# Weight fetches per attention step, route operations behind x, two low halves on GpSimd: one change to a fused attention and mixture-of-experts kernel

## The chip, the cores and the metric

The kernel runs on one core of a Trainium2 chip. The metric is the device time of one execution in microseconds (us). Engines are named as in the profile: PE is TensorE (PEld its weight loads), DVE VectorE, ACT ScalarE, POOL GpSimd, SP SyncE, which issues most of the DMAs.

## The reference

Eight heads of windowed attention (four plain, four dilated by 4, 32 keys for each query) give x, 4608 tokens of 512. Each token then goes to one of 4 groups and one of 4 experts of its group, and its output row is the expert's two-layer FFN times the two gate weights. Cut to what matters:

```python
scores = np.where(masks, q @ k.T / 8, -1e9)             # 8 batches, 8 heads, 576 positions, 64 wide
x = (softmax(scores) @ v)                               # -> (4608, 512)
g_idx = argmax(x @ w_group); g_w = softmax(x @ w_group)[g_idx]
e_idx = argmax(x @ w_expert[g]); e_w = softmax(...)[e_idx]
out[token] = g_w * e_w * (relu(x @ w1[g, e]) @ w2[g, e])   # w1: 512x1024, w2: 1024x512, 16 experts
```

## The kernel before, in words

**Attention** runs in 36 steps (s = 0 to 35, three lagging ones behind), each 64 queries of two batches with all heads; three steps make a group g, nine a pair of batches bp. A step is a pipeline over engines: scores s on PE (mask matmul L253, then 32 small ones L272), maximum mx and difference d on DVE (L282, L284), exp on ACT, transposition t on PE with its copy pt on ACT, the product with the values o on PE (`av`, two steps later, L314), then den, its reciprocal and x = o / den on DVE (`normalise`, L363 to L370), transposition tx and copies xT on ACT. The accumulator of o has one buffer (pool psA), so the next o waits until x has read it. x goes to a table xd in memory (`store_x`); q, k and v of the coming groups are loaded by SP (`load_q`, `load_k` in two halves, `load_v`).

**Routing.** When a pair of batches is through, `turned_logits` forms its logits on PE and `route(bp)`, a generator, picks group and expert of each token, ranks the tokens, and writes slots, tables and gates. Its some 40 DVE operations are small, most 0.2 to 0.35 us. `slot()` is called after each large DVE operation of a step and lets route run on as far as a credit allows. The last things of a route are the gate weights gt (`L554` on ACT, stored by SP at L556), the table of tokens and, for two of the routes, `find`, whose entry list lets GpSimd gather rows of an early expert (`fetch_rows`, tiles xe, L687). Route 2 also picks the second early expert (`pick`).

**Early experts.** The two fullest experts so far are picked after routes 1 and 2, and some of their tokens (128 and 256) are computed while attention and the last route end. `prefetch` drives `load_weights`: the expert's w1 and w2 are 8 chunks of 512 KB. A chunk is fetched by SP into one of four stage buffers w (L641), multiplied by 64 into fp16 by ACT (the high half, L662), and the rest, the low half, is formed either on DVE in one operation (L659) or on GpSimd in two (multiply L656, subtract L657). A chunk's stage buffer is free for the fetch four chunks later when its low half is done; expert 1's chunks 0 to 3 thus take the buffers of expert 0's chunks 4 to 7. `WSTEPS` says how many such pieces run in a step (1 unless named), `EARLY_STEPS` the same for the first expert's FFN, `TAIL` the order of the pieces after the attention loop: r is a piece of the last route, a of expert 0's FFN, b of expert 1's, w of the weights. After that come 16 pieces of experts, whose order is fixed too.

**Order.** PE, DVE, ACT and SP execute what stands here in the order of the code; GpSimd's order is the scheduler's. Each queue is served in order, so an instruction that waits holds all behind it. In the built program SP's transfers use eight semaphores in turn, and each transfer waits until the one eight places ahead of it has landed.

Of the kernel before, what the change touches and what calls it, by code (L numbers as in the profile page):

```python
# [26 lines left out]
NT = NBP * NJ  # L27
# [13 lines left out]
NEARLY = 2  # L41
NWST = 4
RATE = (0.25, 0.3, 0.4)
WSTEPS = {NT - 9: 1, NT - 8: 0, NT + 1: 2, NT + 2: 0}
EARLY_STEPS = {NT - 1: 1, NT: 2, NT + 1: 1}
TAIL = "ararrrarrawrrrawrwarrrrrrwbwarbrwbrrwbrrrwbrrrTwbbb"
NR = NE + NEARLY
# [4 lines left out]
NW = 8192 // WCH  # L52
# [3 lines left out]
def moe_attention_kernel(ctx, tc, q, k, k0, v, cmask, wgate, wpack, out):  # L56
# [174 lines left out]
    routes, gate, credit, rate = [], [], [0.0], [0.0]  # L231
# [5 lines left out]
        for i in range(n):  # L237
            nc.tensor.matmul(t[:, i % 2].rearrange("p (u m c) -> p u m c", u=2, m=2), idb, m, start=True, stop=True)

    def slot():  # L240
        credit[0] = min(credit[0] + rate[0], 2 * rate[0])
        while routes and not gate and credit[0] > 0:
            took = run(routes)
            if took in (2, 3):
                gate.append(took)
            elif took not in (None, 1):
                credit[0] -= took

    def scores(n):
        g, jl, J = n // 3, n % 3, n % NJ  # L250
        s = psS.tile([P, 4, 2, 64], F32, name="s", tag="s")
        m = masks[:, MASK_OF.get(J, 1), :]
        nc.tensor.matmul(  # L253
            s.rearrange("p (t u) w k -> p t (u w) k", t=2),
            idb,
            m.rearrange("p (t k) -> p t k", t=2).unsqueeze(2).broadcast_to([P, 2, 4, 64]),
            start=True,
            stop=False,
        )
        if n < 2:  # L260
            keep_busy((3, 10)[n])
        qv = qb[three(g)][:, jl]
        if n == 0:
            kv, ev0 = k0t[:, :, 0 : 8 * 96].rearrange("p w (s b k) -> p w b s k", s=8, k=32), 2
        else:
            kv, ev0 = kb[g % NK].rearrange("p w (b s k) -> p w b s k", s=8, k=32), 4
        for c in range(4):
            for bb in range(2):
                for a in range(2):
                    sl, j = bb * 4 + c, bb * 2 + a  # L270
                    first, step = jl + a, ev0 - a
                    nc.tensor.matmul(  # L272
                        s[32 * j : 32 * j + 32, c].rearrange("p w k -> p (w k)"),
                        qv[:, (sl * 2 + a) * 32 : (sl * 2 + a) * 32 + 32],
                        kv[:, :, first : first + step + 1 : step, sl],
                        start=False,
                        stop=(c == 3),
                    )
        s = s.rearrange("p c w k -> p (c w) k")
        d = ap.tile([P, 4, 64, 2], F32, name="d", bufs=2)  # L280
        mx = ap.tile([P, 8], F32, name="mx")
        nc.vector.tensor_reduce(mx, s, axis=AX.X, op=ALU.max)  # L282
        slot()
        nc.vector.tensor_tensor(  # L284
            d.rearrange("p c k w -> p c w k"),
            s.rearrange("p (c w) k -> p c w k", w=2),
            mx.rearrange("p (c w) -> p c w", w=2).unsqueeze(3).broadcast_to([P, 4, 2, 64]),
            ALU.subtract,
        )
        slot()  # L290
        dd[n] = d

    def softexp(n):
# [65 lines left out]
    def normalise(n):  # L359
        o = oo.pop(n)  # L360
        ov = o[:, :, 0:260].rearrange("p k (s c) -> p k s c", c=65)
        den = ap.tile([P, 2, 4], F32, name="den")
        nc.vector.tensor_scalar_add(den, ov[:, :, :, 64], 1e-9 / SX)  # L363
        slot()
        nc.vector.reciprocal(den, den)
        slot()
        if n % 3 == 0:
            xg[n // 3] = ap.tile([P, 3, 512], F32, name="x", bufs=2)
        x = xg[n // 3][:, n % 3]
        nc.vector.tensor_tensor(  # L370
            x.rearrange("p (k s c) -> p k s c", k=2, s=4),
            ov[:, :, :, 0:64],
            den.unsqueeze(3).broadcast_to([P, 2, 4, 64]),
            ALU.mult,
        )
        if n % 3 == 2:
            if n < NT - 1:
                store_x(n // 3, (0,))
        elif n % 3 == 0 and n:
            store_x(n // 3 - 1, (1,))  # L380
        st[n] = x.rearrange("p (s w c) -> p s w c", s=4, w=2)
# [247 lines left out]
        nc.vector.tensor_copy(ordi[:, NEARLY:NE], ordf[:, NEARLY:NE])  # L629


    def load_weights(ev, w, aside=lambda i: False):
        src = wpack[bass.ds(ev * P, P), :]

        w32s, depth = {}, len(stages)

        def fetch(i):
            if i < NW:
# [8 lines left out]
        def chunk(i):  # L647
# [4 lines left out]
            if i > 0:  # L652
                w32 = w32s.pop(i - 1)
                h, l = parts(i - 1)
                if aside(i - 1):
                    nc.gpsimd.tensor_scalar(w32, w32, SW, 1.0, ALU.mult, ALU.mult)  # L656
                    nc.gpsimd.tensor_tensor(l, w32, h, ALU.subtract)  # L657
                else:
                    nc.vector.scalar_tensor_tensor(l, w32, SW, h, ALU.mult, ALU.subtract)  # L659
                fetch(i + depth - 1)  # L660
            if i < NW:
                nc.scalar.mul(parts(i)[0], w32s[i], SW)  # L662

        return [lambda i=i: chunk(i) for i in range(-1, NW + 1)]

    def select(ent, which, k0, nt, two):
        sq = sm.tile([P, nt, NE], F32, name=f"sel{nt}")
# [229 lines left out]
    ev, found = {}, []  # L897
# [11 lines left out]
    def prefetch():  # L909
        for r in range(NEARLY):  # L910
            while r not in ev:
                yield
            todo.extend(load_weights(ev[r], wsets[r], lambda i: r == 0 and i not in (4, 6)))
            todo.pop(0)()
            yield
            while not wsets[r]:
# [328 lines left out]
```

## Time and profile before

| | |
|---|---|
| median of 3 runs | 568.92 us (567.52 to 569.07) |
| the profiled execution | 562.74 us |
| its span, first to last instruction | 561.0 us |
| granted clock of PE over the span | 0.996 |
| busy, share of the span | PE 535.4 us (95%), PEld 69%, DVE 66%, ACT 57%, POOL 40% |
| moved by DMA | 134.31 MB, mean 239 GB/s |

The busy share is a mean over stages of different kinds: attention to about 147 us, the early experts with the last route to about 187 us, then the 16 pieces. [...] A releaser is inferred: the engine named is the one that came last by the profile.

### The profile page before, as it was taken

The numbers are of one execution on the slowest core, as the hardware profiler recorded it, in microseconds if no ns is written. First come the engines' busy times: TensorE is split into PE (matmuls) and PEld (weight loads), VectorE is DVE, ScalarE is ACT, GpSimd is POOL, SyncE is SP. The second block draws the span as 40 slices with busy tenths as digits, with TensorE's granted clock in tenths as the row PEclk, the third lists the DMA queues.
The fourth block names the chain that finished last, engine by engine and source line by source line (L and its number), as shares of the span: only waits on it lengthen the run. The fifth ranks groups of instructions, "written<-read, shape, count | busy, mean of one in ns | idle before, by whom it ended". The sixth has DMA issues, their size and how long they took to land.

```text
span 561.0 us, 16459 instructions
## 1 busy us (share of the span) xinstructions
PE 535.4 (95%) x6577; PEld 385.9 (69%) x6577; DVE 370.7 (66%) x846; ACT 317.1 (57%) x563; POOL 223.2 (40%) x211
## 2 busy tenths in 40 slices
PE   6899989997798999999999999999999999999995
PEld 3688878776676676556666666675766756787893
DVE  8776876876777336473868596757657667658650
ACT  6565546575555236464646564656656747647741
POOL 6796665758731423302231614133251421221212
PEclk9999999998999999999999999999999999999999
DMA  8988998798393726958697778779798798897731
GB/s 286 395 285 278 331 275 282 231 315 275 103 316 107 252 68 167 295 162 230 193 292 187 261 193 276 181 249 280 233 302 230 251 327 218 287 327 238 264 103 31
DMA packets 79265, 134.31 MB, mean 239 GB/s; under 512 B 42988, under 2 KB 52630, under 8 KB 79186
## 3 DMA queue, kind: packets, MB, share of 16 engines
q1 hardware_dynamic: 72258, 113.65, 65.7%
q0 software_dynamic: 6784, 19.51, 10.6%
q8 instruction: 53, 0.87, 0.6%
q14 instruction: 26, 0.21, 0.1%
q10 hardware_dynamic: 144, 0.07, 0.0%
HBM read 106.16 MB, written 19.29 MB: 224 GB/s over the span
## 4 chain that ended last, share of the span: by engine, by line
PE 82%; DMA 6%; DVE 5%; issue 2%; ACT 2%; SPq 2%; POOLq 0%; ACTq 0%; DVEq 0%
PE a L748 32%; PE y L841 26%; PE o L314 4%; PE y L859 4%; PE s L272 4%; DMA qb<-q 4%; PE yt L876 3%; PE t L302 3%; DMA kb<-k 2%; PE tx L392 2%; SPq L357 1%; PE lt_ps L417 1%; PE s L253 1%; DMA w<-wpack 1%; DVE wb2l L659 1%
## 5 line engine op out<-in xcount | busy, mean ns | idle before, releaser
L812 POOL DMA_INDIRECT out<-yr,sent x31 | 34.4, 1109 | 220.3 <-ACT yr L811 204.0
L756 DVE SCALAR_TENSOR_TENSOR hl<-a,hh 128x256 f16<-128x256 f32 (+13 forms) x144 | 61.1, 425 | 91.5 <-ACT hh L755 91.3
L748 PE MATMUL a<-xs,wb1h 128*128 128x256 f16 (+7 forms) x576 | 97.8, 275 | 2.5 <-DVE hl L756 2.5
L748 PE MATMUL a<-xs,wa 128*128 128x304 f16 (+7 forms) x864 | 96.6, 272 | 0.0
L755 ACT ACTIVATE hh<-a 128x256 f16<-128x256 f32 (+13 forms) x144 | 55.8, 388 | 63.0 <-PE a L748 62.2
L748 PEld LDWEIGHTS <-wa 128*128 128x128 f16 x864 | 79.2, 98 | 16.4 <-issue 0.2
L841 PEld LDWEIGHTS <-hh 128*128 128x128 f16 x480 | 46.9, 98 | 54.8 <-issue 1.2
L659 DVE SCALAR_TENSOR_TENSOR wa<-w,wa 128x1024 f16<-128x1024 f32 x58 | 69.5, 1217 | 19.1 <-ACT wa L662 19.1
L748 PE MATMUL a<-xs,wb1l 128*128 128x256 f16 (+7 forms) x288 | 78.3, 275 | 0.0
L841 PE MATMUL y<-wa,hh 128*128 128x512 f16 x240 | 73.9, 379 | 0.0
L662 ACT ACTIVATE wa<-w 128x1024 f16<-128x1024 f32 x64 | 66.8, 1055 | 1.5 <-DMA w<-wpack 1.3
L748 PEld LDWEIGHTS <-wb1h 128*128 128x128 f16 x576 | 55.1, 98 | 15.2 <-issue 3.0
L811 ACT ACTIVATE yr<-y,cs 128x512 f32<-128x512 f32 (+3 forms) x31 | 21.3, 687 | 64.4 <-issue 32.1
L687 POOL DMA_INDIRECT xr<-xd,sent x41 | 41.9, 1022 | 29.9 <-DVE sent L675 16.7
L659 DVE SCALAR_TENSOR_TENSOR wb2l<-w,wb2h 128x1024 f16<-128x1024 f32 x32 | 38.3, 1219 | 17.1 <-ACT wb2h L662 17.1
L303 ACT COPY pt<-t 128x512 f32<-128x512 f32 x36 | 21.1, 586 | 44.7 <-PE t L302 44.4
L841 PE MATMUL y<-wb2h,hh 128*128 128x512 f16 x120 | 45.6, 380 | 0.0
L841 PE MATMUL y<-wb2h,hl 128*128 128x512 f16 x120 | 45.5, 379 | 0.0
L841 PE MATMUL y<-wb2l,hh 128*128 128x512 f16 x120 | 45.5, 379 | 0.0
L841 PE MATMUL y<-wa,hl 128*128 128x512 f16 x120 | 45.5, 379 | 0.0
L314 PE MATMUL o<-vs,pt 128*32 128x130 f32 x576 | 40.4, 278 | 3.8 <-POOL wa L657 1.4
L282 DVE TENSOR_REDUCE mx<-s 128x8 f32<-128x512 f32 x36 | 24.6, 685 | 25.0 <-PE s L272 24.8
(206 smaller groups left out, 1073.1 us busy)
## 6 DMA issues: line engine op xcount, KB each, us to landing
w<-wpack SPq DMA_DIRECT2D x128, 512.0 KB, 5.1
kb<-k SPq DMA_DIRECT2D x24, 384.0 KB, 4.6
vt<-v SPq DMA_DIRECT2D x14, 390.0 KB, 7.1
qb<-q SPq DMA_DIRECT2D x7, 768.0 KB, 6.2
xd<-x SPq DMA_DIRECT2D x24, 192.0 KB, 5.8
wa<-v SPq DMA_DIRECT2D x6, 390.0 KB, 7.5
wa<-q SPq DMA_DIRECT2D x3, 768.0 KB, 8.6
xd<-x SPq DMA_DIRECT2D x32, 48.0 KB, 4.4
```

The costliest lines, as they stand in the source:

```text
L272: nc.tensor.matmul(s[32 * j : 32 * j + 32, c].rearrange("p w k -> p (w k)"), qv[:, (sl * 2 + a) * 32 : (sl * 2 + a) * 32 + 32], kv[:, :, f ...
L282: nc.vector.tensor_reduce(mx, s, axis=AX.X, op=ALU.max)
L314: nc.tensor.matmul(o[32 * j : 32 * j + 32, c // 2, at : at + 130], pt[n % NPT][:, c, 32 * j : 32 * j + 32], t[:, :, jl, bb * 4 + c, :], st ...
L659: nc.vector.scalar_tensor_tensor(l, w32, SW, h, ALU.mult, ALU.subtract)
L662: nc.scalar.mul(parts(i)[0], w32s[i], SW)
L687: nc.gpsimd.indirect_dma_start(out=xr[0:n], out_offset=None, in_=xd[0:known, :], in_offset=bass.IndirectOffsetOnAxis(ap=ent[0:n, t : t + 1 ...
L748: nc.tensor.matmul(a[:, 0:cap], ww[:, c * FF + f * P : c * FF + f * P + P], xx[:, c, 0:cap], start=(i == 0), stop=(i == len(mm) - 1),)
L755: nc.scalar.activation(hh[:, f, 0:cap], a[:, 0:cap], AF.Relu)
L756: nc.vector.scalar_tensor_tensor(hl[:, f, 0:cap], a[:, 0:cap], 0.0, hh[:, f, 0:cap], ALU.max, ALU.subtract)
L812: ins = nc.gpsimd.indirect_dma_start(out=out, out_offset=bass.IndirectOffsetOnAxis(ap=ent[0:n, t : t + 1], axis=0), in_=yr[0:n, :], in_off ...
L841: nc.tensor.matmul(yp, h[:, f, t * P : t * P + n], ww[:, f * DM : f * DM + DM], start=(i == 0), stop=(i == len(mm) - 1),)
L859: nc.tensor.matmul(yp[q * (P // g) : q * (P // g) + n, 0:wd], h[:, f, t * P : t * P + n], ww[:, f * DM + q * wd : f * DM + q * wd + wd], s ...
```

## The change

Three things change. Expert 0's weights are no longer fetched four at once in step 27 and one per step from step 30 on; `load_weights` with ahead=2 fetches chunk 0 in step 27, chunk 1 in step 28 and from then on the chunk two places ahead of the one that ACT multiplies. The step without a piece is 34 in place of 28, and step 38 now has one, so the first four fetches of expert 1 are written in step 38 in place of 37. `slot(hold)` lets nothing run in scores from step 34 on and in normalise of steps 34 and later (n of 32 and more); what is owed is run at the slot behind normalise. And chunks 4 and 5 of expert 1 form their low halves on GpSimd, where all eight were on VectorE; expert 0's six stay there.

```diff
--- before.py
+++ after.py
@@ -41,7 +41,9 @@
 NEARLY = 2
 NWST = 4
 RATE = (0.25, 0.3, 0.4)
-WSTEPS = {NT - 9: 1, NT - 8: 0, NT + 1: 2, NT + 2: 0}
+HOLD = NT - 2
+ASIDE = ((0, 1, 2, 3, 5, 7), (4, 5))
+WSTEPS = {NT - 9: 1, NT - 2: 0, NT + 1: 2, NT + 2: 1}
 EARLY_STEPS = {NT - 1: 1, NT: 2, NT + 1: 1}
 TAIL = "ararrrarrawrrrawrwarrrrrrwbwarbrwbrrwbrrrwbrrrTwbbb"
 NR = NE + NEARLY
@@ -237,8 +239,15 @@
         for i in range(n):
             nc.tensor.matmul(t[:, i % 2].rearrange("p (u m c) -> p u m c", u=2, m=2), idb, m, start=True, stop=True)
 
-    def slot():
-        credit[0] = min(credit[0] + rate[0], 2 * rate[0])
+    owed = [0]
+
+    def slot(hold=False):
+
+        owed[0] += 1
+        if hold:
+            return
+        n, owed[0] = owed[0], 0
+        credit[0] = min(credit[0] + n * rate[0], (n + 1) * rate[0])
         while routes and not gate and credit[0] > 0:
             took = run(routes)
             if took in (2, 3):
@@ -280,14 +289,14 @@
         d = ap.tile([P, 4, 64, 2], F32, name="d", bufs=2)
         mx = ap.tile([P, 8], F32, name="mx")
         nc.vector.tensor_reduce(mx, s, axis=AX.X, op=ALU.max)
-        slot()
+        slot(n >= HOLD)
         nc.vector.tensor_tensor(
             d.rearrange("p c k w -> p c w k"),
             s.rearrange("p (c w) k -> p c w k", w=2),
             mx.rearrange("p (c w) -> p c w", w=2).unsqueeze(3).broadcast_to([P, 4, 2, 64]),
             ALU.subtract,
         )
-        slot()
+        slot(n >= HOLD)
         dd[n] = d
 
     def softexp(n):
@@ -361,9 +370,9 @@
         ov = o[:, :, 0:260].rearrange("p k (s c) -> p k s c", c=65)
         den = ap.tile([P, 2, 4], F32, name="den")
         nc.vector.tensor_scalar_add(den, ov[:, :, :, 64], 1e-9 / SX)
-        slot()
+        slot(n >= HOLD - 2)
         nc.vector.reciprocal(den, den)
-        slot()
+        slot(n >= HOLD - 2)
         if n % 3 == 0:
             xg[n // 3] = ap.tile([P, 3, 512], F32, name="x", bufs=2)
         x = xg[n // 3][:, n % 3]
@@ -629,10 +638,11 @@
         nc.vector.tensor_copy(ordi[:, NEARLY:NE], ordf[:, NEARLY:NE])
 
 
-    def load_weights(ev, w, aside=lambda i: False):
+    def load_weights(ev, w, aside=lambda i: False, ahead=None):
         src = wpack[bass.ds(ev * P, P), :]
 
         w32s, depth = {}, len(stages)
+        lead = ahead or depth - 1
 
         def fetch(i):
             if i < NW:
@@ -657,11 +667,13 @@
                     nc.gpsimd.tensor_tensor(l, w32, h, ALU.subtract)
                 else:
                     nc.vector.scalar_tensor_tensor(l, w32, SW, h, ALU.mult, ALU.subtract)
-                fetch(i + depth - 1)
+            if i > 0 or ahead:
+                fetch(i + lead)
             if i < NW:
                 nc.scalar.mul(parts(i)[0], w32s[i], SW)
 
-        return [lambda i=i: chunk(i) for i in range(-1, NW + 1)]
+        whole = [lambda i=i: chunk(i) for i in range(-1, NW + 1)]
+        return [lambda i=i: fetch(i) for i in range(ahead)] + whole[1:] if ahead else whole
 
     def select(ent, which, k0, nt, two):
         sq = sm.tile([P, nt, NE], F32, name=f"sel{nt}")
@@ -910,7 +922,7 @@
         for r in range(NEARLY):
             while r not in ev:
                 yield
-            todo.extend(load_weights(ev[r], wsets[r], lambda i: r == 0 and i not in (4, 6)))
+            todo.extend(load_weights(ev[r], wsets[r], lambda i: i in ASIDE[r], 2 - 2 * r))
             todo.pop(0)()
             yield
             while not wsets[r]:
```

SP, from step 27 on: w is a weight chunk, qb, kb queries and keys of the last group, xd the stores of x and of the gates gt (the ISA row ahead of each w is left out). Before:

```order
L110 DMA qb_108<-q 128x512
L641 DMA w_2174<-wpack 128x1024
L641 DMA w_2176<-wpack 128x1024
L641 DMA w_2178<-wpack 128x1024
L641 DMA w_2180<-wpack 128x1024
L110 DMA qb_108<-q 128x512
L345 DMA xd<-x 64x3x256
L350 DMA xd<-x 48x256
L357 DMA xd<-x 48x2x256
L357 DMA xd<-x 16x3x256
L556 DMA xd<-gt 128x9x16
L114 DMA kb_115<-k 64x1536
```

Now:

```order
L112 DMA qb_108<-q 128x512
L651 DMA w_2174<-wpack 128x1024
L112 DMA qb_108<-q 128x512
L354 DMA xd<-x 64x3x256
L359 DMA xd<-x 48x256
L366 DMA xd<-x 48x2x256
L366 DMA xd<-x 16x3x256
L565 DMA xd<-gt 128x9x16
L651 DMA w_2272<-wpack 128x1024
L116 DMA kb_115<-k 64x1536
```

Three fetches have moved: the second stands behind gt, the third ahead of the last half of kb, the fourth behind the values that follow it.

VectorE, step 34, with route 2 picking the second early expert (own, km, top, ordi are its small tiles). Before:

```order
L282 TENSOR_REDUCE mx<-s 128x8
L577 SCALAR_TENSOR_TENSOR own<-own,low 128x16
L580 SCALAR_TENSOR_TENSOR own<-top,own 128x16
L284 TENSOR_TENSOR d<-s,mx 128x4x2x64
L583 TENSOR_REDUCE km<-own 128x1
L585 TENSOR_TENSOR top<-own,km 128x16
L363 TENSOR_SCALAR den<-o 128x8
L587 TENSOR_TENSOR own<-top,own 128x16
L589 TENSOR_REDUCE km<-own 128x1
L591 CAST ordi<-km 128x1
L593 TENSOR_TENSOR own<-top,own 128x16
L365 RECIPROCAL den<-den 128x8
```

Now:

```order
L291 TENSOR_REDUCE mx<-s 128x8
L293 TENSOR_TENSOR d<-s,mx 128x4x2x64
L372 TENSOR_SCALAR den<-o 128x8
L374 RECIPROCAL den<-den 128x8
L379 TENSOR_TENSOR x<-o,den 128x512
L586 SCALAR_TENSOR_TENSOR own<-own,low 128x16
L589 SCALAR_TENSOR_TENSOR own<-top,own 128x16
L592 TENSOR_REDUCE km<-own 128x1
L594 TENSOR_TENSOR top<-own,km 128x16
L596 TENSOR_TENSOR own<-top,own 128x16
```

The five operations of the attention step now stand together, and all of the route's of this step behind x, ahead of the next mx.

GpSimd, at the end of the attention: chunk 7 of expert 0, the two gathers of expert 1's rows (xe, which read xd), the last route's okm and mv, and the first store of finished rows. Before:

```order
L656 TENSOR_SCALAR w_2681<-w_2681 128x1024
L657 TENSOR_TENSOR wa_92<-w_2681,wa_92 128x1024
L687 DMA xe_224<-xd,ente_231 128x528
L687 DMA xe_225<-xd,ente_231 128x528
L509 TENSOR_TENSOR okm<-okm,mine_214 128x72
L512 TENSOR_TENSOR mv<-E_209,okm 128x576 x2
L812 DMA out<-yr,ente_230 4608x512
L687 DMA xr<-xd,sent 128x528
```

Now:

```order
L699 DMA xe_224<-xd,ente_231 128x528
L666 TENSOR_SCALAR w_2850<-w_2850 128x1024
L699 DMA xe_225<-xd,ente_231 128x528
L667 TENSOR_TENSOR wa_92<-w_2850,wa_92 128x1024
L518 TENSOR_TENSOR okm<-okm,mine_214 128x72
L521 TENSOR_TENSOR mv<-E_209,okm 128x576 x2
L666 TENSOR_SCALAR w_3182<-w_3182 128x1024
L824 DMA out<-yr,ente_230 4608x512
L667 TENSOR_TENSOR wb2l<-w_3182,wb2h 128x1024
L666 TENSOR_SCALAR w_3199<-w_3199 128x1024
L667 TENSOR_TENSOR wb2l<-w_3199,wb2h 128x1024
L699 DMA xr<-xd,sent 128x528
```

Chunk 7's two operations have gone behind the first gather and around the second, and four new ones (wb2l, chunks 4 and 5 of expert 1) stand ahead of the gathers xr. The order of TensorE's instructions is the same in both; on ScalarE the multiplications of chunks 5, 6 and 7 each come one step later, that of chunk 7 now behind gt.

## Rows read from the trace of the kernel before

**Rows 1.** Windows: stretch, length, busy us (instructions) by engine, PEclk, DMA share, GB/s

```profile
112.00:187.00 75.00, 64.87 (x998) 50.60 (x990) 54.77 (x162) 41.53 (x84) 40.94 (x31) 0.98 0.67 215
187.00:561.00 374.00, 368.25 (x3355) 253.10 (x3353) 231.44 (x445) 210.39 (x346) 103.04 (x99) 1.00 0.76 227
...
115.00:120.00 5.00, 4.64 (x119) 4.08 (x119) 3.38 (x9) 2.89 (x6) 1.06 (x2) 1.00 0.96 331
...
131.00:132.00 1.00, 1.00 (x25) 1.00 (x21) 0.58 (x1) 0.00 (x0) 0.93 (x1) 0.50 1.03 328
```

**Rows 2.** TensorE's waits, 112 to 187 us: releaser, us in total, times, longest

```profile
PE a L748 <- DVE hl L756: 2.5, 3, 1.2
PE s L272 <- DMA kb<-k: 2.3, 1, 2.3
PE tx L392 <- DVE own L559: 1.5, 1, 1.5
PE o L314 <- POOL wa L657: 1.4, 1, 1.4
PE o L314 <- DVE own L497: 0.9, 1, 0.9
```

**Rows 3.** Timeline of VectorE: start, duration, line, operation, tiles [idle before, releaser]

```profile
136.47 0.69 DVE L282 TENSOR_REDUCE mx<-s 128x8 f32<-128x512 f32 x1 [0.54 <-PE s L272]
...
140.48 1.23 DVE L659 SCALAR_TENSOR_TENSOR wa<-w,wa 128x1024 f16<-128x1024 f32 x1
...
144.18 0.69 DVE L370 TENSOR_TENSOR x<-o,den 128x512 f32<-128x512 f32 x1 [0.17 <-DMA xd<-x]
...
150.99 0.59 DVE L541 TENSOR_SCALAR s<-s 128x45 f32<-128x45 f32 x1
...
172.16 0.19 DVE L541 TENSOR_SCALAR s<-s 128x45 f32<-128x45 f32 x1
```

**Rows 4.** Timeline of SP's DMA issues, 111 to 127 us

```profile
111.69 2.15 SPq L641 DMA_DIRECT2D w<-wpack  x4
...
126.32 0.49 SPq L114 DMA_DIRECT2D kb<-k  x1
```

**Rows 5.** The tile kb, 95 to 150 us, its transfers

```profile
DMA to landing us min/median/max: 3.4/3.6/4.3
```

**Rows 6.** Timeline of TensorE: masks of steps 32, 33, 34; t of step 35

```profile
124.01 0.38 PE L253 MATMUL s<-masks,idb 128*128 128x512 bf16 x1
...
127.15 0.38 PE L253 MATMUL s<-masks,idb 128*128 128x512 bf16 x1
...
135.01 0.38 PE L253 MATMUL s<-masks,idb 128*128 128x512 bf16 x1
...
146.43 0.66 PE L302 MATMUL t<-id,d 128*128 128x128 f32 x4 [0.31 <-DVE xs L725]
```

**Rows 7.** Timeline of SP's DMA issues, 152 to 165 us

```profile
152.87 0.38 SPq L556 DMA_DIRECT2D xd<-gt  x1
...
155.79 0.58 SPq L345 DMA_DIRECT2D xd<-x  x1
...
164.40 0.36 SPq L641 DMA_DIRECT2D w<-wpack  x1
```

**Rows 8.** Timeline of GpSimd, 140 to 157 us

```profile
140.86 1.76 POOL L656 TENSOR_SCALAR w<-w 128x1024 f32<-128x1024 f32 x1 [1.41 <-ACT wa L662]
...
150.21 1.33 POOL L656 TENSOR_SCALAR w<-w 128x1024 f32<-128x1024 f32 x1 [2.94 <-ACT wa L662]
...
155.91 1.09 POOL L687 DMA_INDIRECT xe<-xd,ente  x1 [2.16 <-DVE hl L756]
```

**Rows 9.** Timeline of ScalarE, 168 us: chunk 4 of expert 1

```profile
168.05 1.06 ACT L662 ACTIVATE wb2h<-w 128x1024 f16<-128x1024 f32 x1 [2.54 <-DMA w<-wpack]
```

**Rows 10.** Lines 656 and 657: duration ns min/median/max, first and last start

```profile
L656 POOL TENSOR_SCALAR w<-w x6: 1037/1055/1757, 118.9 to 150.2; 128x1024 f32<-128x1024 f32 x6
...
L657 POOL TENSOR_TENSOR wa<-w,wa x6: 2124/2135/2153, 120.0 to 151.6; 128x1024 f16<-128x1024 f32 x6
```

## The prediction

> **What bounds the kernel now.** I read the stretches first. From 187 us on TensorE is busy 368.25 of 374 us [rows 1]: there it is the bound, and a shift of what stands before 187 us comes out at the end one to one. Between 112 and 187 us it is busy 64.87 of 75 us [rows 1], so 10.1 us at most are to be had, and the change touches this stretch alone. The list of TensorE's waits there [rows 2] has five large entries: 2.5 us for the low halves hl of the early experts' first layer, 2.3 for keys (kb), 1.5, 1.4 and 0.9 around x. The two named "own" and "POOL wa" are, by the program, waits for x: psA has one buffer, so the o of a step can't start before the x of the step before has been read out of it. The x of 144.18 us ends at 144.87 [rows 3], and the o named for 1.4 us starts 0.15 us later.
>
> Two chains cross here. The attention chain ends at the store of the gates of route 2 (gt, L556). Behind that store, in order on SP, stand the first four fetches of early expert 1, and the conversion of its chunks bounds TensorE up to 181 us. So I follow gt, not TensorE, through the change.
>
> **Part 1, one fetch per step.** In before, four fetches go out from 111.69 us on [rows 4]. SP's transfers use eight semaphores in turn, each waiting for the landing of the one eight places earlier; so what follows waits for chunk after chunk, and the second half of the last keys leaves only at 126.32 [rows 4]. It lands some 3.4 us later (3.4 to 4.3 is the spread, [rows 5]) and TensorE waits 2.3 us for it [rows 2]. After that idle time the granted clock is 0.50 at 131 to 132 us [rows 1], the lower of the two levels. Step 33 thus takes 7.86 us from mask to mask, where step 32 took 3.14 [rows 6]: 4.7 more, 2.3 of it the wait, about 1.6 the low clock (some three us at 0.5 to 0.7), the rest the matmuls of the rank, which step 32 doesn't have. In the new order three fetches (1.5 MB) are gone from ahead of the first kb half, one only stands between it and the second, and each of the issues costs SP about 0.55 us as before. I put the second half's issue at 122.5 to 123.5 and its landing at 126 to 128; step 33 wants it at 127.5. The wait is then 0 to 0.8 us. I take 0.4, and the low clock gone: **-3.5 us** at step 34 (bounds -4.0 and, if it lands no earlier, 0). What covers the fetches: each chunk is multiplied by ScalarE two steps after its fetch is written, and SP runs one to two steps behind TensorE, so chunks 2 to 4 may come up to 1.5 us after ScalarE is ready for them; the pt copy queued behind that multiply has 0.8 to 1 us of slack before the o that needs it, since the next scores stand ahead of that o. I cost it at nothing, up to 0.6 us if late. The stage buffers allow it: low 0 is done before chunk 4 is fetched.
>
> **Part 2, route operations behind x.** In step 34 eleven small operations that stood between mx and x now stand behind x, with two that were there already. The o that follows gains the 0.9 us. But the thirteen, 0.2 us each, are all ahead of the next mx: mx of step 35 comes 0.1 + 0.8 + 0.6 + 0.2 + 0.2 + 0.6 + 2.6 = 5.1 us after the scores (the distances of mx, d, den, rec, x and thirteen small ones), no earlier than now, while the 1.23 us low half of 140.48 [rows 3] and two more route operations leave the way of the x behind it. From the mx of step 34 at 136.47 [rows 3] to the t of step 35 at 146.43 [rows 6] it was 9.96 us; in the new order I add up 9.45: **-0.5 us**, not the 2.6 us that the waits sum to, because VectorE's 5.1 us per step are more than TensorE's 3.14. From that t to the gt store at 152.87 it is 6.44 us [rows 6, 7]; x goes first now, but the sums for gt follow it, and the low half that stood ahead of them (1.2) goes behind: no difference. The 1.5 us before tx disappears, yet what it fed (the last logits) is not late next. gt thus leaves at 152.87 - 4.0 = 148.9.
>
> **Part 3, what stands behind gt.** SP: fetches 1 to 3 of expert 1, then fetch 4, whose stage buffer is that of chunk 7 of expert 0. In before that chunk's multiply ran at 150.21 and its subtract right behind it [rows 8], done at 153.7, so all four were out before the store of 155.79 [rows 7]. In the new order chunk 7's two GpSimd operations stand behind the first gather of expert 1's rows and around the second. That gather started 3.04 us after the gt store (152.87 to 155.91, [rows 7, 8]), it has to see the gates landed, and this doesn't change. So: 148.9 + 3.0, gather 1.2, multiply 1.05, 0.3 of issue, second gather 1.0, subtract 2.14 [rows 10], with 0.2 of gaps = 157.8 us for fetch 4, against some 155.3: **2.5 us later although gt is 4 earlier**. Behind it SP has eight stores of x, 0.6 us each [rows 7], then chunk 4 of expert 1: 157.8 + 0.5 + 4.9 + 0.2 = 163.4. In before it left at 164.40, held by the landing of the first store of 155.79, eight places ahead, which lay behind 2 MB of weights. Now only 0.5 MB lies ahead of that store, so the issue time decides: **-1.0 us**. ScalarE waited for this chunk until 168.05 [rows 9], 3.65 us after its fetch, and the first relu of expert 1 stands behind that on ScalarE, ahead of everything that TensorE waits for next; it moves by -0.9. That expert 1's first fetches are now written in step 38 changes nothing: they stand behind gt on SP either way.
>
> **Part 4, two low halves on GpSimd.** VectorE gives up 2 x 1.2 = 2.4 us between 170 and 174 us; GpSimd takes on 2 x (1.055 + 2.135) = 6.4 us [rows 10], from about 168 to 176, where it was idle and before its gathers of the next rows. If the engines didn't touch, TensorE's 2.5 us of waits for hl would shrink only by 0.4: the gt of route 3 and then chunk 7's multiply still stand ahead of the fourth relu on ScalarE. But they do touch. GpSimd's multiply of 140.86 took 1.76 us instead of 1.055 while VectorE's low half of 140.48 to 141.71 ran [rows 3, 8], and VectorE's add L541 of 150.99 took 0.59 us, against 0.19 at 172.16 with GpSimd idle, ending with GpSimd's multiply of 150.21 to 151.54 [rows 3, 8]. In the new order that add (at about 171.1) meets a subtract of 170.7 to 172.85: +1.0 behind it at the hl. The two low halves left on VectorE (at 174 and 177) stand beside the second chunk's subtract; nothing in the trace shows a VectorE low half that waits for GpSimd, only the reverse and the add. Bounds: -0.4 with no waiting, +0.6 with the add alone, +2.15 if both low halves wait. I take one of them waiting, **+1.25**, since the two directions that rows show make it likely and the two instructions become ready within 0.1 us of each other.
>
> [...]
>
> **Sum.** -0.9 + 1.25 = +0.35 us at the end of expert 1's first layer, and TensorE is the bound from there on. Span 561.0 + 0.35 = 561.35; the profiled execution took 562.74, 1.74 more than its span, so 563.1. The median of the three runs is 568.92, 6.2 us above the profiled one; I carry the difference over: **569.3 us**. About 0.3% (1.7 us) is what a measurement can tell from no change.
>
> **Rivals.** (a) The attention's gain survives. If the fourth fetch doesn't hold expert 1 (the gather starts on its entry list rather than on the landed gates, or GpSimd's two operations get in front), all behind gt moves by 4.0 and part 4 gives back 0.5: -3.5, 565.4 us. For it: SP and TensorE really are freed. Against it: GpSimd's order is fixed in the program and the 3.04 us are in the trace. 0.25. (b) Slower: the keys come no earlier, because the DMA engines were 96% busy from 115 to 120 us [rows 1] and the same bytes have to pass; then gt gains only 0.5 to 1, fetch 4 leaves near 161.3, chunk 4 at 166.8, +2.4, and part 4 adds 0.6: +3.0, 572 us. It decides as soon as gt gains less than 3.0 us, for then chunk 4 leaves later than 164.4. For it: the low halves' reordering costs 6.4 us on that path and is certain; the gain that pays for it isn't. 0.23. (c) The clock: TensorE would sit idle 1.7 to 1.8 us twice between 162 and 170, waiting for xs and for the first hl. It fell to the lower level only after 2.3 us [rows 1, 2]; if it does there, +1.6 on top, 571 us. 0.07. (d) My forecast, 0.45: near nothing, because the gain of one chain is spent by the next.
>
> **How the numbers follow.** (d) spans roughly 567.5 to 570.7, mostly within 0.3% of 568.92; (a) lies below, (b) and (c) above. Faster by over 0.3%: 0.25 + 0.02 = 0.27; slower by over 0.3%: 0.23 + 0.07 = 0.30; within: 0.43. For 8 in 10 the range reaches into (a) and (b): 565.8 to 572.0.
>
> **What would show it.** Step by step: the wait of TensorE's scores for kb under 1 us and the clock at 1.0 from 127 to 135; the o of step 35 behind its scores without a wait; gt of route 2 on SP near 149; GpSimd's subtract of chunk 7 ending 8.5 to 9 us behind it and the fourth fetch of expert 1 right then; chunk 4's fetch at 163 to 164; VectorE's second-route add lengthened to over 1 us, a low half beside GpSimd's subtract over 2. I am wrong if fetch 4 leaves before 155, if the kb wait stays, or if the waits for hl fall by more than 1 us.

## The result, and the profile after

The changed kernel takes 570.59 us (median of 12 runs), the kernel before 568.92 (12 runs beside them). The ratio on record is **1.0056, 95% interval 1.0031 to 1.0081**: 3.2 us slower, with 1.8 to 4.6 inside the interval. The two medians by themselves differ by only 1.7 us (0.3%), just under that interval, so the size of the loss is less sure than its sign; below, the price of a whole kernel in us is its ratio times 569. The forecast was +0.4 us, with 0.43 on "within 0.3%". By the ratio the loss lies closest to rival (b), +3.0. Rival (c) is near in size, but the clock that it spoke of (TensorE's granted clock, PEclk below, as a share of full speed) stayed at 1.00 from 162 to 177 us, counted from the span's start like every point in time below. The profiled execution took 573.22 us with a span of 571.5.

The two spans, 561.0 and 571.5, differ by 10.5 us, and that is not the change. From the first layer-2 matmul of early expert 1 (y) to the end, where TensorE is the bound (busy 368.25 of 374 us from 187 us on, [rows 1]), the profile of before has 379.5 us and that of after 383.4. A second profile of the unchanged kernel before has 384.6 there (last section). So what the change did has to be read in pieces that don't contain that stretch: **mask of step 27 to mask of step 34** (the keys), **mask of step 34 to the store of route 2's gates, gt** (the end of attention), **gt to y of expert 1** (the first expert's conversion).

The windows of the changed kernel that answer to [rows 1]: stretch, length, busy us (instructions) by engine, PEclk, DMA share, GB/s.

```profile
112.00:187.00 75.00, 60.42 (x992) 48.89 (x990) 54.77 (x146) 42.14 (x85) 44.76 (x33) 0.95 0.69 211
...
145.00:146.00 1.00, 0.29 (x8) 0.32 (x12) 1.00 (x3) 1.00 (x4) 0.22 (x1) 0.77 0.10 27
146.00:147.00 1.00, 1.00 (x25) 1.00 (x21) 1.00 (x4) 1.00 (x2) 0.92 (x2) 0.50 0.84 187
```

And TensorE's waits from 112 to 190 us, answering to [rows 2].

```profile
PE a L760 <- DVE hl L768: 5.6, 4, 2.1
PE s L281 <- DMA kb<-k: 3.2, 2, 2.9
PE lt_ps L426 <- DVE tab L573: 1.9, 1, 1.9
PE o L323 <- DVE okm L511: 1.8, 1, 1.8
```

The wait before tx (1.5) is gone and another stands in its place: lt_ps, 1.9. The waits for hl have risen from 2.5 to 5.6, and the wait for keys has not gone. The next three timelines (start, duration, engine, line, operation, tiles, and in brackets the idle time before) show each in turn. First SP's issues around the last keys and behind gt, which answer to [rows 4, 7], and the scores of TensorE that waited.

```profile
119.15 0.77 SPq L651 DMA_DIRECT2D w<-wpack  x1
120.03 0.85 SPq L116 DMA_DIRECT2D kb<-k  x1
...
124.37 0.36 SPq L651 DMA_DIRECT2D w<-wpack  x1
124.77 0.49 SPq L116 DMA_DIRECT2D kb<-k  x1
...
154.66 0.38 SPq L565 DMA_DIRECT2D xd<-gt  x1
155.29 8.37 SPq L651 DMA_DIRECT2D w<-wpack  x4
...
168.91 1.07 SPq L651 DMA_DIRECT2D w<-wpack  x2
```

```profile
131.43 1.55 PE L281 MATMUL s<-kb,qb 128*32 128x128 f32 x32 [2.87 <-DMA kb<-k]
```

The second half of the keys left 1.5 us earlier than in before, yet the scores could start only 6.7 us later (3.55 in before). Its transfer met busier DMA engines: the windows around it are, in before and in the changed kernel (the last two figures are the DMA share and GB/s),

```profile
126.00:130.00 4.00, 1.65 (x26) 1.09 (x20) 2.46 (x9) 2.95 (x7) 3.72 (x4) 1.00 0.71 184
```

```profile
124.00:131.00 7.00, 4.56 (x86) 3.73 (x84) 5.39 (x16) 3.45 (x7) 3.66 (x3) 1.00 1.01 335
```

Behind gt the four fetches are one piece of 8.37 us, since the fourth waits for its buffer until 163.3; chunk 4's fetch follows at 168.91, 14.25 us behind gt (11.53 before). GpSimd shows why, and VectorE shows what two of GpSimd's operations do; they answer to [rows 8] and [rows 3].

```profile
157.69 1.08 POOL L699 DMA_INDIRECT xe<-xd,ente  x1 [4.95 <-DVE hl L768]
158.81 1.06 POOL L666 TENSOR_SCALAR w<-w 128x1024 f32<-128x1024 f32 x1
160.05 1.08 POOL L699 DMA_INDIRECT xe<-xd,ente  x1 [0.17 <-issue]
161.16 2.14 POOL L667 TENSOR_TENSOR wa<-w,wa 128x1024 f16<-128x1024 f32 x1
...
176.53 2.14 POOL L667 TENSOR_TENSOR wb2l<-w,wb2h 128x1024 f16<-128x1024 f32 x1
178.62 1.05 POOL L666 TENSOR_SCALAR w<-w 128x1024 f32<-128x1024 f32 x1
179.76 2.13 POOL L667 TENSOR_TENSOR wb2l<-w,wb2h 128x1024 f16<-128x1024 f32 x1
```

```profile
176.92 2.80 DVE L550 TENSOR_SCALAR s<-s 128x45 f32<-128x45 f32 x1
179.76 0.19 DVE L553 TENSOR_TENSOR es<-s,own 128x36 f32<-128x36 f32 x1
...
180.77 2.20 DVE L669 SCALAR_TENSOR_TENSOR wb2l<-w,wb2h 128x1024 f16<-128x1024 f32 x1
```

The add L550 (L541 before), 0.19 us long in before, sat through the rest of a subtract and through the multiply behind it, until 179.7. The low half of 180.77 sat through the next subtract: 2.20 us instead of 1.22.

### The profile page after: what moved, and what is told of

Read it like the earlier page. It is cut to its first block, busy times and chain, and to the rows that moved or that the text cites. A ratio compares the mean times of both kernels' runs of the same rounds, so it can differ in the third digit from the quotient of the medians.

```text
span 571.5 us, 16462 instructions
## 1 busy us (share of the span) xinstructions
PE 539.2 (94%) x6577; PEld 387.4 (68%) x6577; DVE 373.8 (65%) x844; ACT 315.8 (55%) x563; POOL 233.9 (41%) x215
## 3 DMA queue, kind: packets, MB, share of 16 engines
q0 software_dynamic: 6784, 19.51, 10.5%
## 4 chain that ended last, share of the span: by engine, by line
PE 77%; DMA 10%; DVE 4%; SPq 3%; issue 3%; ACT 1%; POOL 1%; POOLq 0%; DVEq 0%; ACTq 0%
PE a L760 31%; PE y L853 26%; PE y L871 4%; PE o L323 4%; DMA xd<-x 3%; PE yt L888 3%; PE s L281 3%; DMA kb<-k 3%; DMA qb<-q 3%; PE t L311 2%; PE tx L401 1%; SPq L366 1%; DMA w<-wpack 1%; SPq L359 1%; SPq L354 1%
## 5 line engine op out<-in xcount | busy, mean ns | idle before, releaser
L824 POOL DMA_INDIRECT out<-yr,sent x31 | 39.1, 1261 | 216.9 <-ACT yr L823 199.9
L669 DVE SCALAR_TENSOR_TENSOR wb2l<-w,wb2h 128x1024 f16<-128x1024 f32 x30 | 36.8, 1254 | 13.2 <-ACT wb2h L673 7.7
```

What stands on the lines that cost most here:

```text
L824: ins = nc.gpsimd.indirect_dma_start(out=out, out_offset=bass.IndirectOffsetOnAxis(ap=ent[0:n, t : t + 1], axis=0), in_=yr[0:n, :], in_off ...
```

## The experiments

Two theories stood at the start. **Theory 1 (order)**, the forecast's part 3 with its rival (b): the keys come no earlier, and chunk 7's GpSimd pair behind the gather delays expert 1's fourth fetch. **Theory 2 (waits)**: the two GpSimd pairs hold VectorE up, as a GpSimd multiply did with the add in before (0.59 us instead of 0.19, [rows 3, 8]), and that is the loss. A third, that holding route operations costs, came from the first runs.

Each ratio below is to runs of before beside them, with its 95% interval. The intervals reach some 2 us to either side, so a difference of 1 or 2 us between two kernels is not shown by their ratios alone. The table has the three stretches of one profiled execution each. "Keys" is from the mask of step 27 to that of step 34; the mask rows are those of line 253, or 262 in the kernels built on the changed one.

| kernel | keys | 34 to gt | gt to y | ratio |
|---|---|---|---|---|
| before | 30.92 | 17.86 | 28.61 | 1 |
| before, again | 31.10 | 17.86 | 29.54 | 1 |
| changed | 31.32 | 18.09 | 33.43 | 1.0056 |
| changed, again | 29.11 | 18.12 | 33.66 | 1.0049 |
| fetch alone | 28.29 | 16.81 | 31.60 | 0.9979 |
| hold alone | 30.73 | 23.07 | 29.26 | 1.0060 |
| lows alone | 28.17 | 17.85 | 32.02 | 1.0054 |
| changed, no lows | 28.28 | 17.50 | 32.79 | 0.9995 |
| changed, no hold | 31.05 | 15.96 | 34.41 | 1.0031 |
| changed, old fetch | 31.80 | 22.11 | 32.42 | 1.0073 |
| changed, chunk 7 on VectorE | 29.23 | 17.48 | 33.54 | 1.0016 |
| changed, no add | 31.27 | 17.98 | 31.88 | 1.0003 |
| fetch and chunk 7 | 28.98 | 16.62 | 29.75 | 0.9956 |
| the same again | 28.99 | 16.92 | 29.76 | 0.9962 |
| the same, lows, no add | 28.43 | 15.85 | 32.64 | 0.9991 |
| the same, step 29 skipped | 28.32 | 17.72 | 31.43 | 1.0000 |
| fetch late | 27.26 | 24.35 | 30.11 | 1.0050 |

Nearly all kernels are the changed one with some of these four edits, which undo a part each (the lows, the hold, the fetches in two lines) or all but one, so that a part stands alone:

```diff
-ASIDE = ((0, 1, 2, 3, 5, 7), (4, 5))
+ASIDE = ((0, 1, 2, 3, 5, 7), ())
-HOLD = NT - 2
+HOLD = NT + 9
-WSTEPS = {NT - 9: 1, NT - 2: 0, NT + 1: 2, NT + 2: 1}
+WSTEPS = {NT - 9: 1, NT - 8: 0, NT + 1: 2, NT + 2: 0}
-lambda i: i in ASIDE[r], 2 - 2 * r)
+lambda i: i in ASIDE[r])
```

**One part undone.** The lows back on VectorE (the first edit):

> The changed kernel with the last part undone: the low halves of chunks 4 and 5 of early expert 1 are on VectorE again, everything else as changed. The yardstick is the time from the store of route 2's gates (gt) to the first layer-2 matmul (y) of expert 1: 28.6 us before, 33.4 us in the changed kernel. Theory 1 (order: the fourth fetch of expert 1 stands behind chunk 7's GpSimd pair, which stands behind the gather): chunk 4's fetch still leaves some 14 us behind gt, gt to y is 32 to 33, and the time stays at 1.003 to 1.005 of before. [...]

0.9995 (0.9963 to 1.0028). The add and the low half are back at their old lengths:

```profile
174.37 0.19 DVE L550 TENSOR_SCALAR s<-s 128x45 f32<-128x45 f32 x1
...
176.73 1.16 DVE L669 SCALAR_TENSOR_TENSOR wb2l<-w,wb2h 128x1024 f16<-128x1024 f32 x1
```

The time went back to that of before, as theory 2 has it, and gt to y (32.8) stayed as theory 1 has it: both delays exist, and one partly covers the other. The time fell by more than the stretches account for, 1.4 us of some 3 without the keys; the intervals (1.0028 above here, 1.0031 below for the changed kernel) leave that open. Chunk 4's fetch still left 14.6 us behind gt.

The hold undone (the second edit):

> The changed kernel with the second part undone: route operations run between mx and x in the last steps again. If part 2 is a gain of 0.5 us as forecast, the time rises to 1.006 to 1.007 of before and the o of step 35 waits for x again. If holding the operations back is what lost the time (gt came 7.05 us behind the t of step 35, 6.44 before), gt stands 0.6 us earlier behind that t and the time falls to 1.004 or less. Theories 1 and 2 both expect the first.

1.0031 (0.9999 to 1.0064): not slower than the changed kernel, and gt comes 16.0 us behind the mask of step 34 instead of 18.1. That was the first sign that the hold doesn't gain.

The fetches undone (the last two edits):

> The changed kernel with the first part undone: expert 0's chunks are fetched in the old burst and steps again, the held route operations and the two more low halves on GpSimd stay. Chunk 7's GpSimd pair then stands ahead of both gathers again. Theory 1 (order): fetch 4 leaves at 2.5 us behind gt, chunk 4's at 11 to 12, gt to y is 29 to 30.5, time 1.000 to 1.002 of before. [...] The second half of the last keys leaves late again (126.3 us or so) and TensorE waits 2.3 us for it, by both.

1.0073 (1.0033 to 1.0112), the slowest of all. The hold with the old fetches costs 4.2 us ahead of gt, so the time is no test of the theories; gt to y is. The order on GpSimd was mended (chunk 4's fetch left 12.7 us behind gt), and gt to y was still 32.4: theory 1 alone can't be.

Chunk 7 of expert 0 on VectorE (`ASIDE = ((0, 1, 2, 3, 5), (4, 5))`):

> The changed kernel with one more edit: the low half of chunk 7 of expert 0 is VectorE's, so that fetch 4 of expert 1 needs neither the gather nor the GpSimd pair behind it. Theory 1 (order): fetch 4 leaves within 4 us of gt instead of 8.7, chunk 4's within 10 to 11 instead of 14.2, gt to y falls from 33.4 to 30 to 31, time 1.000 to 1.002 of before. [...]

1.0016 (0.9981 to 1.0051). The fetches left together 0.6 us behind gt and chunk 4's 12.3 behind it, but the add now took 3.72 us, since it began 0.5 us ahead of the subtract that it then sat through, and gt to y stayed at 33.5: what the order gave, the wait for GpSimd took.

**Profiles once more.** The kernel before:

> The kernel before, unchanged, profiled once more. From the first layer-2 matmul (y) of expert 1 to the end of the span it took 379.5 us in the first profile, and 383.4 to 384.6 in the changed kernel and four variants of it, though TensorE's program is the same there. If this is a difference of the kernels, it is 379.5 again; if it is one of the executions, 383 to 385. The second half of the last keys leaves at 126 to 127 us, and step 33 takes 7.5 to 8.5 us from mask to mask by both.

384.6 us from y to the end: not a difference of the kernels. The keys left at 128.3 and step 33 took 8.2.

The changed kernel:

> The changed kernel, unchanged, profiled and timed beside the next two. In three variants with the same fetch order the second half of the last keys left at 122.9 to 123.7 us and step 33 took 4.5 to 5.6 us from mask to mask; in the first profile of the changed kernel 124.8 and 8.4. If that was one execution's chance, step 33 takes 4.5 to 6 us here and the gates of route 2 (gt) leave at 149 to 152 us instead of 154.7; if the changed kernel can't do it, 8 us and 154 to 155. The time is 1.003 to 1.008 of before by all theories.

1.0049 (1.0006 to 1.0092). Step 33 took 4.63 us this time, gt left at 153.5. The first profile of after was unlucky in its keys: of the ten profiles with the new fetches only it and one other have a step 33 over 8 us.

**One part alone.** The lows (all edits but the first):

> The kernel before with the last part of the change alone: the low halves of chunks 4 and 5 of early expert 1 on GpSimd. [...] Theory 1 (order): 1.000 to 1.002.

1.0054 (1.0011 to 1.0097). With no other part in, the add takes 3.71 us, and the small operations behind it do not wait. VectorE, then GpSimd:

```profile
173.28 3.71 DVE L550 TENSOR_SCALAR s<-s 128x45 f32<-128x45 f32 x1
177.02 0.19 DVE L553 TENSOR_TENSOR es<-s,own 128x36 f32<-128x36 f32 x1
...
177.69 0.17 DVE L558 TENSOR_TENSOR own<-own,s 128x9 f32<-128x9 f32 x1
...
178.03 2.20 DVE L669 SCALAR_TENSOR_TENSOR wb2l<-w,wb2h 128x1024 f16<-128x1024 f32 x1
```

```profile
172.69 1.08 POOL L824 DMA_INDIRECT out<-yr,ente  x1 [0.18 <-ACT hh L767]
173.80 2.13 POOL L667 TENSOR_TENSOR wb2l<-w,wb2h 128x1024 f16<-128x1024 f32 x1
175.89 1.05 POOL L666 TENSOR_SCALAR w<-w 128x1024 f32<-128x1024 f32 x1
177.03 2.12 POOL L667 TENSOR_TENSOR wb2l<-w,wb2h 128x1024 f16<-128x1024 f32 x1
```

The add began during GpSimd's indirect store, before the subtract, and ends 0.05 us behind the multiply; the low half ends 1.08 behind the second subtract. Alone, this part costs what the whole change costs.

The fetches (the first two edits):

> The kernel before with the first part of the change alone: expert 0's chunks fetched one per step. Theory 1 (order): gt of route 2 leaves 1 to 2 us earlier than before, but chunk 4's fetch 14 us behind it instead of 11.5, time 1.001 to 1.004 of before. [...]

0.9979 (0.9937 to 1.0020). Chunk 4's fetch is 14.3 us behind gt as forecast, gt to y +2.5 us, and yet the time isn't worse, since gt is earlier. The interval holds no change and a gain of up to 3.6 us.

The hold (all edits but the second):

> The kernel before with the second part of the change alone: route operations held behind x in the last steps. From the mask of step 34 to the store of gt it took 17.86 us before, 16.0 and 16.8 with the new fetches and no hold, 17.5 to 18.1 with both, 22.1 with the hold and the old fetches. Theory 3 (holding costs: all held operations stand ahead of the next mx): 21 to 22 us again, gt 3 to 4 us late, time 1.003 to 1.007 of before. Forecast as on record (holding gains 0.5 us): 17.4 us, time 0.998 to 1.000.

1.0060 (1.0025 to 1.0094): theory 3. VectorE and the wait of TensorE in this kernel:

```profile
141.32 1.66 DVE L669 SCALAR_TENSOR_TENSOR wa<-w,wa 128x1024 f16<-128x1024 f32 x1
142.91 0.68 DVE L291 TENSOR_REDUCE mx<-s 128x8 f32<-128x512 f32 x1
```

```profile
PE o L323 <- DVE okm L511: 3.3, 1, 3.3
```

The mx of step 35 in before:

```profile
141.62 0.68 DVE L282 TENSOR_REDUCE mx<-s 128x8 f32<-128x512 f32 x1
```

The thirteen held operations and then the low half all stand ahead of the mx of step 35, which comes 7.95 us behind the mask of step 34 (6.61 in before), and the o of step 36 waits 3.3 us for the x behind it. Set between mx, d, den and rec the operations partly overlap with these: from mx of step 34 to the last of them (the cast to hl) it was 3.9 us in before and is 4.8 here, and the low half, 1.66 instead of 1.23, adds the other 0.4. That is 1.3 of the 5.2 us by which gt is late. Two more things came with it: behind the wait of 3.3 us the granted clock was 0.50 from 145 to 149 us (1.00 in before, where that wait is 1.44 [rows 2]), and the add of route 2 now met GpSimd's subtract and took 1.86 us instead of 0.59. One of the windows:

```profile
147.00:148.00 1.00, 1.00 (x14) 0.61 (x7) 0.32 (x2) 0.19 (x1) 1.00 (x2) 0.50 0.00 0
```

**What combines.** One fetch per step, chunk 7 on VectorE, no hold, no lows (`ASIDE = ((0, 1, 2, 3, 5), ())` and the second edit):

> The first part of the change alone, and the low half of chunk 7 of expert 0 on VectorE, so that neither the gather nor the GpSimd pair stands between gt and the fourth fetch of expert 1. The first part alone gave 0.998 of before with 31.6 us from gt to the first y of expert 1 (28.6 and 29.5 in the two profiles of before). If the order of GpSimd costs those 2 to 3 us, it is 29 to 30 here, and the time 0.992 to 0.996 of before. If something else holds chunk 4 (the issue of the stores on SP, or the last logits, which waited 2.2 to 3.3 us for their table in two of the variants), it stays at 31 to 32 and the time at 0.997 to 1.000.

0.9956 (0.9918 to 0.9993), and once more, beside other kernels:

> The kernel of the best run so far once more, one fetch per step with chunk 7 of expert 0 on VectorE and nothing else of the change: 0.993 to 0.998 of before if its gain of 0.4% is real, 0.998 to 1.002 if it was chance; gt to y 29.5 to 30 us.

0.9962 (0.9927 to 0.9997). This kernel beats both, by some 2.3 us. SP in the first of them:

```profile
147.68 0.38 SPq L565 DMA_DIRECT2D xd<-gt  x1
148.31 2.76 SPq L651 DMA_DIRECT2D w<-wpack  x4
```

The four fetches take 2.76 us instead of 8.4, chunk 4's leaves at 159.84 (12.2 behind gt), and gt to y is 29.75: the order cost 1.85 us of the 31.6 with the fetches alone.

The changed kernel without the add:

```diff
-        nc.vector.tensor_scalar_add(s5, s5, 1e-9)
```

> The changed kernel without the add of 1e-9 to the sums (L550; they are 1 or more, so it changes no bit of them), which took 2.80 us beside GpSimd's subtract and multiply. [...] If the add is only a place where VectorE stands while something else is late, gt to y stays at 33 and the time at 1.005.

1.0003 (0.9969 to 1.0038), gt to y 31.9 instead of the 33.4 and 33.7 of the changed kernel, as theory 2 has it. The keys waited 2.9 us in this profile.

One fetch per step, chunk 7 on VectorE, lows on GpSimd, no add:

> One fetch per step, chunk 7 of expert 0 on VectorE, no held operations, the two more low halves on GpSimd, and the add of 1e-9 left out (it changes no bit). Only VectorE's own low halves can now wait for GpSimd. If the add was the whole price of the two pairs, gt to y is 29 to 29.7 us as without them and the time as in the next run, 0.994 to 0.997. If the low halves pay in its place (2.2 us instead of 1.2, once or twice), gt to y is 30.5 to 32 and the time 1 to 2 us above the next run, 0.997 to 1.000.

0.9991 (0.9956 to 1.0026), gt to y 32.6: the second of the two, and a little above its 32. VectorE's own low halves pay now:

```profile
173.16 2.73 DVE L668 SCALAR_TENSOR_TENSOR wb2l<-w,wb2h 128x1024 f16<-128x1024 f32 x1
...
176.79 2.16 DVE L668 SCALAR_TENSOR_TENSOR wb2l<-w,wb2h 128x1024 f16<-128x1024 f32 x1
```

**The keys.** No fetch in step 29 (`NT - 7: 0` in WSTEPS in place of `NT - 2: 0`), with chunk 7 on VectorE:

> As the run with chunk 7 on VectorE, but no weight chunk is fetched in step 29, so that none is issued between the two halves of the last keys. If the transfers ahead of it decide when the second half lands, it leaves at 121 to 122 us instead of 123 to 125 and lands 2 us or more earlier, TensorE's wait for keys (0.5 to 2.9 us in five profiles of the new fetches) is 0, step 33 takes 4.4 to 4.7 us from mask to mask, and the time is 0 to 0.003 below that run. If the engines are full anyway, the wait is as before and the time the same.

1.0000 (0.9963 to 1.0037). The second half left at 121.2, and the scores still waited 1.3 us, to 6.05 us behind the issue: the chunk right ahead of it isn't what holds it. The time did not fall below that of the same kernel with step 29 (0.9956 and 0.9962), as was expected.

No fetch before step 30 (`NT - 6: 1`, and 2 in steps 35 and 36):

> The first part alone, with the first weight chunk fetched in step 30 instead of 27, behind the second half of the last keys on SP; steps 35 and 36 issue one more piece each to catch up. No weight chunk is then ahead of the keys. With the new fetches the second half left at 121.2 to 125.3 us and took 5.6 to 6.8 us to land, against 3.4 in the kernel before. Counted from the mask of step 27, the scores that wait for it started at 25.6 to 26.9 us before and at 24.6 to 26.2 with the new fetches. If the bytes ahead of it decide (rival b), it lands at 22 to 24 here, the wait is 0 and step 33 takes 4.2 to 4.7 us. If something else holds it (the buffer of the keys, SP's other transfers), it stays at 24.5 to 26. The time is no test: the chunks come three steps late, 0.995 to 1.010.

Here no chunk is ahead of the keys, which left at 120.6 and landed 4.5 us later, 21.2 us behind the mask of step 27, and the wait is 0:

```profile
126.95 0.38 PE L262 MATMUL s<-masks,idb 128*128 128x512 bf16 x1
127.26 1.08 PE L281 MATMUL s<-kb,qb 128*32 128x128 f32 x32
```

Step 33 took 4.18 us. So the chunks ahead of the keys decide, taken together, and not the one right ahead of them: with three ahead the scores that waited started 25.4 us behind that mask, with two 24.8, with none the keys had landed at 21.2. That it is their bytes, on engines that are full, fits the shares above (0.96 [rows 1], 1.01); no run separates the bytes from the turns that the chunks take on SP. The time, 1.0050 (1.0014 to 1.0085), goes with chunks that come three steps late: gt came 24.35 us behind the mask of step 34.

## Why the prediction was wrong, step by step

| step | forecast | measured |
|---|---|---|
| part 1, keys to the mask of step 34 | -3.5 (0 to -4.0) | -1.0 |
| part 2, mask of step 34 to gt | -0.5 | 0.0 |
| parts 3 and 4, gt to y | +4.35 | +4.4 |
| sum | +0.35 | +3.4 (by the ratio: +3.2) |

The measured column compares means: keys 30.5 us over five profiles with the old fetches and 29.5 over the ten with the new ones (without the runs of step 29 and of the late fetch); 17.86 and 17.83 us to gt (before, twice, and lows alone; five profiles with the new fetches and the hold); 29.1 and 33.5 us to y (before, twice, and hold alone; the changed kernel twice). The keys scatter by 3 us from one execution to the next, 28.2 to 31.8, so that -1.0 is a rough figure.

- **Part 1 is the step that failed.** The issue came as forecast: 19.3 us behind the mask of step 27 instead of 22.1, 2.8 earlier (the forecast's 122.5 to 123.5 against 126.3). The landing didn't follow: from issue to scores it took 5.7 to 6.8 us in the nine of these ten profiles in which they waited, not the 3.4 to 4.3 of [rows 5], and the scores started 25.4 us behind that mask instead of 25.8, a gain of 0.4. The landing times of [rows 5] were read in a kernel whose engines have room by the time the keys leave (share 0.71 from 126 to 130 us), and carried into one where they have none (1.01 from 124 to 131). The count of chunks was off too: two fetches, not three, are gone from ahead of the first half (the one at 119.15 still stands there), and ahead of the second half stand three chunks instead of four. Rival (b) named this cause, and its point of decision, gt gaining less than 3.0 us, is where the case fell (1.0). The low clock that the -3.5 contained should have hung on the landing, not on the issue: step 33 took 5.7 us on average with the new fetches and 7.4 with the old ones, over 7.8 with the clock down (0.50, from 132 to 135 us in the changed kernel) in four of five old profiles and two of ten new ones. So step 33 itself gained 1.8; steps 27 to 32 ahead of it took 23.8 us instead of 23.1, 0.3 of it from one profile. That is where the forecast put the late chunks at nothing; whether late chunks are the cause is not shown.
- **Part 2** hid a gain and a loss in one term. The new fetches alone bring gt to 16.4 us behind the mask of step 34 (five profiles), 1.4 earlier: the low half of 140.48 leaves the way, and mx of step 35 comes 1.2 us sooner; the hold takes the 1.4 back. The forecast credited the low half's absence to the hold. From mx of step 34 to t of step 35 it was 9.59 us, against 9.45 forecast; from t to gt 7.05 instead of 6.44, where "no difference" was said. In three of the five profiles with hold and new fetches the wait ahead of the o of step 36 ended in the low clock (0.50 in both profiles of the changed kernel), and gt came at 18.0 to 18.1 us; in the two others it stayed up (1.00 with the lows back), and gt came at 17.5. Alone on the old fetches the hold costs 4 to 5 us ahead of gt, part of it by the clock (above). That the clock would fall here no term of the forecast had; rival (c) had it behind 162 us.
- **Part 3 was right, in mechanism and size.** Fetch 4 left 8.67 us behind gt (8.9 forecast), chunk 4's fetch 5.58 behind fetch 4 (5.6).
- **Part 4 was right in mechanism and too small.** The add took 2.80 us, not 1.2, because it met two of GpSimd's operations in a row and waited for both; one low half waited, 1.0, as taken. Alone, from the old order, the part costs 3 us: gt to y goes from 29.1 to 32.0, above the bound of 2.15. In the changed kernel chunk 4's delay covers some of it. That parts 3 and 4 together came out at 4.4 us, as forecast, is partly luck: alone they cost 2.5 and 2.9, and what part 4 was short of, the overlap of the two took away.
- **Adding up hid the signs.** The parts alone are -1.2 (fetches), +3.4 (hold) and +3.1 us (lows) by their ratios; with the fetches in, the hold's price is some 0.9 us (0.9995 against 0.9979) and the lows' 3.0 (1.0031 against 0.9979). That gives 2.7 of the 3.2 us, each with some 2 us to either side. The sum's first term alone carried the forecast, and it was the least certain one.

Beside GpSimd's operations the add took 2.80 us (changed kernel) and 3.71 (lows alone) and the low halves 2.16 to 2.73, against 0.19 and 1.16 to 1.22 with the lows back on VectorE: these waited for GpSimd. The small two-input operations didn't: L558 took 0.17 us at 177.69, inside a subtract of 177.03 to 179.15, in the run with the lows alone.

## What to carry to other kernels

The time from issue to landing that was read for the keys, 3.4 to 4.3 us with the DMA engines at a share of 0.71, was 5.7 to 6.8 us to the scores where the share was 1.01: before you credit an earlier issue, ask how many bytes are then still in flight ahead of it. Work moved to GpSimd to relieve VectorE has to be placed against VectorE's instructions that wait for it, down to an add of 45 elements: this one took 2.80 and 3.71 us instead of 0.19, up to the end of the GpSimd operations that followed each other there without a gap. And small operations that fill the gaps of a dependent chain are partly hidden where they are: here the stretch with them took 3.9 us set between the chain's operations and 4.8 gathered, and with the low half that followed them the next turn of the chain came 1.3 us later.

## What the runs showed of the hardware

- **A short VectorE operation waited for a row of GpSimd operations, up to the first gap.** The add of 128x45 took 0.19 us alone, 2.80 beside a subtract's rest and a multiply (changed kernel), 3.71 where it began during the indirect store ahead of the two (lows alone). It did not get in between subtract and multiply, where the one's start and the other's end touch (the multiply of 178.62 starts before the subtract of 176.53 has ended, at 178.67). It did get in behind each multiply, ahead of the subtract that uses its result and starts 0.08 to 0.09 us later: in before it ended at 151.58, between 151.54 and 151.62. A reduce to 128x9 and a two-input operation of that size ran through inside a subtract at 0.17 to 0.20 (before, changed kernel, lows alone).
- **The chips of these runs differed where TensorE is the bound.** From y of expert 1 to the end it was 379.5 to 380.1 us in all seven profiles of one chip and in the first profile of before (no chip is on record for the first profiles of before and after), and 383.4 to 385.4 in the others, whatever the kernel. The kernel before, timed beside the others, took 565.1 and 564.2 us on that chip and 569.3 and 569.8 on the two others. In that stretch the first profile of before has no waits of TensorE at all, and the second has these, from 190 us on, nearly all with no other engine's work at their end:

```profile
PE a L748 <- issue: 1.0, 2, 0.6
PE a L748 <- SPq L1159: 0.9, 1, 0.9
PE y L859 <- issue: 0.7, 2, 0.5
PE y L841 <- issue: 0.2, 1, 0.2
```

They make 2.8 us of the 5; the cause stays open. So a span from that chip isn't set here against one from the others; the stretches up to y are.
- **The clock fell after 1.76 us of idle time, and once not after 2.1.** Ahead of the o of step 36 TensorE waited 1.76 us in the changed kernel, and the granted clock was 0.50 behind it (the windows at 146 us above), so that o took 1.96 us instead of 1.09; in before the wait there was 1.44 [rows 2] and the clock stayed at 1.00. A wait of 2.1 us for hl at 178 us left it at 1.00, and so did 1.67 us ahead of the same o in the run with the lows back. That the clock falls only behind more than 2.3 us of idle, as rival (c) had it, doesn't hold.
